# Moving the probability transposes of a fused attention and MoE kernel to float32r operands

## The chip, the cores and the metric

The program runs on one core of one Trainium2 chip. The metric is the device time of one execution in microseconds (us); smaller is better. The kernel before takes 770.42 us (median of three runs, 769.28 to 771.31).

## The reference

Attention over 2 batches, 8 heads, 768 positions and head size 64, in which a query sees only the keys whose 6-bit hash bucket equals its own; then a layer `g = h - tanh(h)` and a gated layer. In the core of it:

```python
mask = q_bucket[:, :, :, None] == k_bucket[:, :, None, :]
scores = np.where(mask, scale * np.matmul(q, k.transpose(0, 1, 3, 2)), -1000000000.0)
scores = scores - np.max(scores, axis=-1, keepdims=True)
attn = np.exp(scores)
attn = attn / (np.sum(attn, axis=-1, keepdims=True) + 1e-09)
x = np.matmul(attn, v)          # regrouped to 1536 tokens x 512
h = x @ w_in; x = (h - np.tanh(h)) @ w_out
g = x @ w_gate; out = (g * (1.0 / (1.0 + np.exp(-g))) * (x @ w_val)) @ w_out2
```

## The kernel before, in words

**Attention** takes the first 245 us or so of the span. The work is cut into 96 steps: 8 pairs of heads, 2 halves of the queries (384 columns each, `TB`), 2 heads of the pair, 3 blocks of 128 queries. `declare_step` declares one step:

- four score matmuls on TensorE (L835; float32r, 384 columns each) into one of two score buffers in PSUM (`s`), which already hold the mask;
- the row maximum on VectorE (L845), the exponential with the row sum on ScalarE (L847; it writes the probabilities into one of four slots `p`), the reciprocal of the sum (L851 on VectorE or GpSimd, L853 on VectorE), and the scaling of the slot in place on GpSimd (L854);
- six transposes of 128x128 on TensorE (L865, the function `transposes`): three into each of the two PSUM buffers `t`. A block of the slot is the stationary operand, an identity matrix of 128 columns is the moving one. Slot, identity and output are float32;
- two copies out of `t` into `pt`, on ScalarE or VectorE (L871).

Every six steps, `declare_pv` issues the product with `v` (L888, plain float32, 24 records for one half of a pair, in two bundles of 12). Its result goes to the feature tiles by L894. Beside the steps run the preparation of the next pair (hash matmul L798, one-hot matmul L832, L769, L787, the moves L745) and the blocks of the next layer's input (L550, L552, L557).

The slots `p` are the first 8 columns-blocks of one long tile, `ct_a`, which also holds the feature tiles from block `XF` = 8 on and is used again later by the matmuls of the layers (`ct_t`). In the profile all of these are called `ct`, and the identity is part of `csb`, which two DMAs of GpSimd's queue fill (L1157).

**The layers** follow: products of a Strassen-like scheme in float32r (L1044, 384 columns) and the second matmuls (L1098, 384 or 512 columns). Their weights arrive as 64-bit values and are converted by VectorE, GpSimd and ScalarE (L462 to L513); that begins while attention still runs.

**Order.** `Plan.order` takes each engine's list of operations from a table of numbers written into the file (`ORDER`). An engine works its list strictly in that order and waits where an operand isn't ready. On TensorE a step's transposes stand behind the scores of later steps, with bundles of the product with `v` in between. The operation as it is declared:

```python
op({"PE": 0.3275 * (1.0, SLOW)[i < 4]}, transposes, r=[pk, "ident"], w=[("t", z)], lat=0.2)
```

The number in it is the planner's cost of three transposes; where the table decides, it moves nothing.

Of the kernel before, what the change touches and what calls it, by code (L numbers as in the profile page):

```python
# [8 lines left out]
F32 = mybir.dt.float32  # L9
F32R = mybir.dt.float32r  # L10
# [4 lines left out]
ALU = mybir.AluOpType  # L15
# [3 lines left out]
NB, NH, S, D = 2, 8, 768, 64  # L19
NBITS = 6  # L20
NPAIR = NH // 2
TB = 384
# [10 lines left out]
NG, NC, NT = 16, 6, 11  # L33
# [13 lines left out]
def chunk_keys():  # L47
# [150 lines left out]
    POOL="""  # L198
# [34 lines left out]
class Plan:  # L233
# [15 lines left out]
    def op(self, eng, fn, r=(), w=(), due=0.0, lat=None, late=False, after=0.0, alt=None, port=()):  # L249
        n = len(self.ops)  # L250
        deps = set()
        for k in r:
            deps.update(self.writers.get(k, ()))
        for k in w:
            deps.update(self.writers.get(k, ()))
            deps.update(self.readers.get(k, ()))
        for k in r:
            self.readers.setdefault(k, []).append(n)
        for k in w:
            if k in r:  # L260
                self.writers.setdefault(k, []).append(n)
            else:
                self.writers[k] = [n]
                self.readers[k] = []
        deps.discard(n)
        self.banks[n] = {k[:2] for k in (*r, *w) if k[0] == "s"}
        eng = {e: t * (1 if e == "PE" or not self.n_first else self.SAFE) for e, t in eng.items()}
        self.ops.append((eng, fn, deps, due, self.LAT if lat is None else lat, late, after,
                         ALT if alt is None else alt, port, self.PE_WAIT if "PE" in eng else 0.0))
# [100 lines left out]
def lsh_attention_moe_kernel(ctx: ExitStack, tc: tile.TileContext, qT, kT, vP, proj, cst, wts, out):  # L370
    nc = tc.nc
    eng = {"PE": nc.tensor, "DVE": nc.vector, "ACT": nc.scalar, "POOL": nc.gpsimd, "SP": nc.sync}
    plan = Plan()
    op = plan.op

    def tiles(stack, name, n, shape, dtype=F32, **kw):
        pool = stack.enter_context(tc.tile_pool(name=name + "_p", bufs=n, **kw))
        return [pool.tile(shape, dtype, tag=name, name=name) for _ in range(n)]
# [10 lines left out]
    pw = fs[:, 2 * S:].bitcast(BF16).rearrange("p (j c) -> p j c", j=4)  # L389
# [11 lines left out]

    op_a = tiles(ctx, "op", 1, [128, 28 * TB], F32R)[0]
    op_t = [op_a[:, i * TB:(i + 1) * TB] for i in range(28)]
    ct_a = tiles(ctx, "ct", 1, [128, (NC + NT + 2) * TB])[0]
    ct_t = [ct_a[:, i * TB:(i + 1) * TB] for i in range(NC + NT + 2)]
    p_t = [ct_a[:, i * S:(i + 1) * S] for i in range(4)]
    XF = 8
    at = ExitStack()
    const = at.enter_context(tc.tile_pool(name="const", bufs=1))
    csb = const.tile([128, 262], F32, name="csb")  # L410
    ident = csb[:, 0:128]
    ones_b = csb[:, 128:129]
    bias_b = csb[:, 129:130]
    pj = const.tile([128, 32], F32, name="pj")
    x_t = tiles(ctx, "x", 1, [128, 512], space=PSUM)
    h_t = tiles(ctx, "h", 1, [128, 512], space=PSUM)
# [2 lines left out]
    t_t = tiles(ctx, "t", 2, [128, 512], space=PSUM)  # L419
# [5 lines left out]
    def ring(name, n):  # L425

        c = counts[name] = counts.get(name, -1) + 1
        return name, c % n
# [166 lines left out]
    def xf_at(half, p, n=1):  # L595
        return ct_a[:, (XF + 4 * half + p) * TB:(XF + 4 * half + p + n) * TB]

# [7 lines left out]
        return "xf", BLOCK[name][0], BLOCK[name][1] + k  # L605

    def tmp_at(ks):
        return ct_a[:, (NC + NT + ks[0]) * TB:(NC + NT + ks[0] + len(ks)) * TB]

    def tmp_key(k):  # L610
        return "tmp", k
# [4 lines left out]
    m_t = tiles(at, "m", 4, [128, 1])  # L616
    sm_t = tiles(at, "sm", 4, [128, 1])
    r_t = tiles(at, "r", 4, [128, 1])
# [203 lines left out]
    def declare_step(i, oh=None):  # L822
        n, half, e, qt = steps[i]
        sk = ring("s", 2)
        s = s_t[sk[1]]
        a, b, qk = ops_of["q", n, e, half]
        ks = [ops_of["k", n, e, kh] for kh in range(2)]
        q0 = slice(qt * 128, qt * 128 + 128)

        def qk_mm(g):  # L830
            if oh:
                g.matmul(out=h_t[0][:, 0:TB], lhsT=pw[:, 2 * oh[0] + oh[1], :], rhs=oh[2][0], start=True, stop=True)  # L832
            for first in (True, False):
                for kh in range(2):
                    g.matmul(  # L835
                        out=s[:, kh, 0:TB], lhsT=(b, a)[first][:, q0], rhs=ks[kh][0 if first else 1],
                        start=first, stop=not first,
                    )

        op({"PE": (0.87 if oh else 0.7) * (1.0, SLOW)[i < 6]}, qk_mm, r=qk + ks[0][2] + ks[1][2] + ([oh[2][1], "pw"] if oh else []),  # L840
           w=[sk + (0,), sk + (1,)] + ([("h", 0)] if oh else []), lat=0.25)
        sv = s[:, :, 0:TB]
        mk, smk, rk, pk = ring("m", 4), ring("sm", 4), ring("r", 4), ring("p", 4)
        m, sm, r, p = m_t[mk[1]], sm_t[smk[1]], r_t[rk[1]], p_t[pk[1]]
        op({"DVE": 0.87}, lambda g: g.tensor_reduce(out=m, in_=sv, axis=AX.XY, op=ALU.max, negate=True),  # L845
           r=[sk + (0,), sk + (1,)], w=[mk])
        op({"ACT": 0.9}, lambda g: g.activation(  # L847
            out=p.rearrange("p (a b) -> p a b", a=2), in_=sv, func=ACTF.Exp, bias=m, accum_out=sm
        ), r=[sk + (0,), sk + (1,), mk], w=[pk, smk])

        op({"DVE": 0.17, "POOL": 0.3}, lambda g: g.tensor_scalar(  # L851
            out=r, in0=sm, scalar1=1e-9, scalar2=None, op0=ALU.add), r=[smk], w=[rk])
        op({"DVE": 0.15}, lambda g: g.reciprocal(out=r, in_=r), r=[rk], w=[rk])  # L853
        op({"POOL": 0.91}, lambda g: g.tensor_scalar(  # L854
            out=p, in0=p, scalar1=r, scalar2=1.0, op0=ALU.mult, op1=ALU.mult
        ), r=[pk, rk], w=[pk])
        if qt == 0:
            pt_k[n, half, e] = ring("pt", 4)
        ptk = pt_k[n, half, e]
        pt = pt_t[ptk[1]]  # L860

        for z in range(2):
            def transposes(g, z=z):
                for kt in range(3):
                    g.transpose(out=t_t[z][:, kt * 128:(kt + 1) * 128], in_=p[:, z * TB + kt * 128:z * TB + (kt + 1) * 128], identity=ident)  # L865

            op({"PE": 0.3275 * (1.0, SLOW)[i < 4]}, transposes, r=[pk, "ident"], w=[("t", z)], lat=0.2)
            dst = pt[:, 3 * z:3 * z + 3, qt * 128:(qt + 1) * 128]
            src = t_t[z][:, 0:TB].rearrange("p (c q) -> p c q", c=3)
            op({"ACT": 0.4, "DVE": 0.47}, lambda g, dst=dst, src=src:  # L870
               g.activation(out=dst, in_=src, func=ACTF.Copy) if g is nc.scalar else g.tensor_copy(dst, src),  # L871
               r=[("t", z)], w=[ptk + (qt, z)])
# [39 lines left out]
        return i, k, w  # L912

    def ct_first(i):
        return [("p", i // 2)] if i < 8 else [("xf", (i - XF) // 4, (i - XF) % 4)] if i < 16 else []

    def c_slot():
        i, k, w = slot("c", NC, range(NC), ct_first)
        return ct_t[i], k, w
# [11 lines left out]
    def stage(layer, m):  # L931

        if m == 0:
            stages[layer] = ring(("st", layer), (2, 4)[layer - 1])[1]
        r = stages[layer]
        key = "st", layer, r, m
        size = (TB, DM)[layer - 1]
        first = []
        if key not in used:
            used.add(key)  # L940
            if layer == 1:
                first = [("xf", r, m)]
            else:
                first = [("acc", r // 2, 4 * (r % 2) + k) for k in range(m * DM // TB, ((m + 1) * DM - 1) // TB + 1)]
        if layer == 1:
            at_ = lambda n=1: ct_a[:, (8 + 4 * r + m) * TB:(8 + 4 * r + m + n) * TB]
        else:
            at_ = lambda n=1: late["acc"][r // 2][:, (r % 2) * 1536 + m * DM:(r % 2) * 1536 + (m + n) * DM]
        return at_, key, first
# [126 lines left out]
    def out_group(layer, i, sb, j):  # L1076
# [71 lines left out]
        if layer == 1 and i == NP1 - 1 and j == 7:  # L1148
            x_blocks(sb, [0, 1], lambda name, ks: acc_at(sb, ACC[name] + ks[0], len(ks)), lambda name, k: ("acc", sb, ACC[name] + k),
                     tmp_at, tmp_key, e + ZDUE[sb], True, MIX, 3)  # L1150
# [2 lines left out]
    MIX = [lambda n: {"DVE": dve(n), "POOL": pool(n)}] * 11  # L1153

    op({"ACT": 0.4}, lambda g: g.dma_start(out=pj, in_=proj), w=["pj"], due=-10, lat=2.5)
    for key, c in (("csb", slice(128, 262)), ("ident", slice(0, 128))):
        op({"POOL": 0.8}, lambda g, c=c: g.dma_start(out=csb[:, c], in_=cst[:, c]), w=[key], due=-10, lat=4.0)  # L1157

    def make_pw(g):
        for j in range(4):  # L1160
            g.tensor_scalar(
                out=pw[:, j, :], in0=csb[:, 130:258], scalar1=csb[:, 258 + j:259 + j], scalar2=None, op0=ALU.mult,
            )

    op({"DVE": 0.9}, make_pw, r=["csb"], w=["pw"], due=-5)
# [15 lines left out]
    for i in range(nst):  # L1181
        n, r = divmod(i, 12)
        m = (i + HASH_STEP) // 12
# [23 lines left out]
    for _, n, m in sorted(slots):  # L1207
        name, i, sb = units[n]
# [91 lines left out]
```

## Time and profile before

| | us |
|---|---|
| median of three runs | 770.42 (769.28 to 771.31) |
| profiled execution, first to last instruction (span) | 768.9 |
| TensorE busy | 754.3 |
| VectorE busy | 602.5 |
| ScalarE busy | 452.1 |
| GpSimd busy | 353.7 |

One execution was profiled. Its span is listed; what lay around the span in that same execution is not, so the difference from the median, 1.5 us, stands for it. Busy times are of records whose ends are modelled for matmuls, and a matmul's record overlaps with the next one's, so TensorE's share says that matmuls follow one another, not how closely. How closely is read from the distance between starts, or from the length of a bundle in the chain of waits, where overlaps are taken out. In the rows below PE is TensorE's matmul side, PEld its weight loads, DVE is VectorE, ACT ScalarE and POOL GpSimd.

### The profile page before, as it was taken

The numbers are of one execution on the slowest core, as the hardware profiler recorded it, in microseconds if no ns is written. First come the engines' busy times: TensorE is split into PE (matmuls) and PEld (weight loads), VectorE is DVE, ScalarE is ACT, GpSimd is POOL, SyncE is SP. The second block draws the span as 40 slices with busy tenths as digits, with TensorE's granted clock in tenths as the row PEclk, the third lists the DMA queues.
The fourth block names the chain that finished last, engine by engine and source line by source line (L and its number), as shares of the span: only waits on it lengthen the run. The fifth ranks groups of instructions, "written<-read, shape, count | busy, mean of one in ns | idle before, by whom it ended". The sixth has DMA issues, their size and how long they took to land.

```text
span 768.9 us, 12367 instructions
## 1 busy us (share of the span) xinstructions
PE 754.3 (98%) x4342; PEld 664.9 (86%) x4342; DVE 602.5 (78%) x1077; ACT 452.1 (59%) x955; POOL 353.7 (46%) x390
## 2 busy tenths in 40 slices
PE   7999999999999999999999999999999999999997
PEld 4677677776767999999999999999999998999896
DVE  6878777888897668888587889997785767789465
ACT  5787788878876646555555546656455443454220
POOL 5665657867785743223233353744135543323010
PEclk9999999999999999999999999999999999999999
DMA  6564465356323016788585763422347665587303
GB/s 172 140 182 93 128 180 137 91 131 176 120 83 110 29 27 174 170 191 198 120 191 123 194 146 91 107 88 91 124 147 185 147 121 140 126 187 159 78 14 150
DMA packets 37133, 101.09 MB, mean 131 GB/s; under 512 B 4656, under 2 KB 10032, under 8 KB 37072
## 3 DMA queue, kind: packets, MB, share of 16 engines
q1 hardware_dynamic: 28288, 71.06, 30.3%
q0 software_dynamic: 8320, 28.45, 20.9%
q10 hardware_dynamic: 464, 0.80, 0.5%
q8 instruction: 34, 0.56, 0.3%
q14 instruction: 27, 0.22, 0.1%
HBM read 49.17 MB, written 15.73 MB: 84 GB/s over the span
## 4 chain that ended last, share of the span: by engine, by line
PE 87%; DVE 4%; DMA 2%; ACT 2%; POOL 2%; issue 1%; SPq 0%; ACTq 0%; DVEq 0%; POOLq 0%
PE bs L1044 30%; PE t L1098 16%; PE s L835 8%; PE h L1098 8%; PE x L888 8%; PE t L865 7%; PE x L1098 6%; PE x L1044 2%; PE t L1044 2%; ACT ct L847 1%; POOL ct L854 1%; DMA q<-in_qT 1%; PE h L1044 1%; DMA raw<-in_w 1%; DVE ct L961 1%
## 5 line engine op out<-in xcount | busy, mean ns | idle before, releaser
L1044 PE MATMUL bs<-x,wi 128*128 128x384 f32 x1200 | 230.8, 335 | 1.4 <-DVE ct L1027 1.4
L1044 PEld LDWEIGHTS bs<-x,wi 128*128 128x128 f32 x1200 | 210.5, 188 | 6.2 <-DVE ct L1027 1.7
L854 POOL TENSOR_SCALAR ct<-ct,r 128x768 f32<-128x768 f32 x96 | 94.0, 983 | 30.5 <-DVE r L853 14.5
L845 DVE TENSOR_REDUCE m<-s 128x1 f32<-128x768 f32 x96 | 91.0, 952 | 20.9 <-PE s L835 19.4
L847 ACT ACTIVATE ct<-s,m 128x768 f32<-128x768 f32 x96 | 86.5, 902 | 17.7 <-DVE m L845 7.1
L835 PE MATMUL s<-op 128*128 128x384 f32 x384 | 91.7, 363 | 2.6 <-ACT ct L847 2.3
L1024 ACT ACTIVATE ct<-bs 128x384 f32<-128x384 f32 x120 | 57.0, 490 | 53.6 <-PE bs L1044 52.4
L865 PE MATMUL t<-csb,ct 128*128 128x128 f32 x576 | 82.1, 275 | 2.3 <-POOL ct L854 1.6
L865 PEld LDWEIGHTS t<-csb,ct 128*128 128x128 f32 x576 | 66.7, 140 | 18.5 <-POOL ct L854 5.5
L835 PEld LDWEIGHTS s<-op 128*128 128x128 f32 x384 | 63.7, 189 | 19.0 <-ACT ct L847 10.8
L871 ACT ACTIVATE pt<-t 128x384 f32<-128x384 f32 x133 | 61.2, 489 | 26.3 <-PE t L865 25.6
L1098 PE MATMUL t<-op,wo 128*128 128x384 f32 x384 | 75.7, 335 | 0.0
L888 PE MATMUL x<-pt,v 128*64 128x384 f32 x384 | 69.0, 495 | 0.0
L1098 PEld LDWEIGHTS t<-op,wo 128*128 128x128 f32 x384 | 67.2, 188 | 0.6 <-DVE ct L1129 0.3
L1098 PE MATMUL t<-wo,op 128*128 128x512 f32 x264 | 67.1, 393 | 0.0
L1137 POOL DMA_DIRECT2D acc<-ct x24 | 21.0, 887 | 78.7 <-ACT ct L1129 39.5
L1098 PEld LDWEIGHTS t<-wo,op 128*128 128x128 f32 x264 | 49.0, 188 | 8.3
L476 POOL TENSOR_TENSOR wi<-fs,wi 128x512 fp32r<-128x512 f32 (+1 forms) x25 | 39.8, 1595 | 25.9 <-ACT wi L474 25.8
L961 POOL TENSOR_TENSOR op<-ct,op 128x384 fp32r<-128x384 f32 x29 | 31.9, 1138 | 42.1 <-ACT op L966 32.9
L961 POOL TENSOR_TENSOR ct<-ct 128x384 f32<-128x384 f32 x24 | 26.4, 1100 | 52.8 <-ACT ct L980 31.9
L888 PEld LDWEIGHTS x<-pt,v 128*64 128x64 f32 x384 | 24.7, 136 | 28.6 <-issue 28.4
L474 ACT ACTIVATE wi<-fs 128x512 fp32r<-128x512 f32 (+1 forms) x60 | 41.8, 701 | 12.4 <-DVE fs L494 4.2
(170 smaller groups left out, 1412.1 us busy)
## 6 DMA issues: line engine op xcount, KB each, us to landing
raw<-in_w SPq DMA_DIRECT2D x68, 512.0 KB, 3.5
acc<-ct POOLq DMA_DIRECT2D x24, 768.0 KB, 6.3
out<-acc POOLq DMA_DIRECT2D x12, 768.0 KB, 8.1
op<-raw SPq DMA_DIRECT2D x42, 192.0 KB, 3.0
op<-f SPq DMA_DIRECT2D x56, 96.0 KB, 3.0
v<-in_v SPq DMA_DIRECT2D x8, 384.0 KB, 4.1
out<-acc SPq DMA_DIRECT2D x4, 768.0 KB, 4.6
acc<-out SPq DMA_DIRECT2D x4, 768.0 KB, 5.1
```

The costliest lines, as they stand in the source:

```text
L474: op({"ACT": act(n)}, lambda e: e.activation(out=hi, in_=src, func=ACTF.Copy), r=rk, w=[wk + (0,)], due=due, late=late)
L835: g.matmul(out=s[:, kh, 0:TB], lhsT=(b, a)[first][:, q0], rhs=ks[kh][0 if first else 1], start=first, stop=not first,)
L845: op({"DVE": 0.87}, lambda g: g.tensor_reduce(out=m, in_=sv, axis=AX.XY, op=ALU.max, negate=True), r=[sk + (0,), sk + (1,)], w=[mk])
L847: op({"ACT": 0.9}, lambda g: g.activation(out=p.rearrange("p (a b) -> p a b", a=2), in_=sv, func=ACTF.Exp, bias=m, accum_out=sm), r=[sk + ...
L854: op({"POOL": 0.91}, lambda g: g.tensor_scalar(out=p, in0=p, scalar1=r, scalar2=1.0, op0=ALU.mult, op1=ALU.mult), r=[pk, rk], w=[pk])
L865: g.transpose(out=t_t[z][:, kt * 128:(kt + 1) * 128], in_=p[:, z * TB + kt * 128:z * TB + (kt + 1) * 128], identity=ident)
L871: g.activation(out=dst, in_=src, func=ACTF.Copy) if g is nc.scalar else g.tensor_copy(dst, src),
L888: g.matmul(out=x[r, :], lhsT=v[:, kt, r], rhs=pt_t[ptks[e][1]][:, kt, :], start=(kt == 0), stop=(kt == NKT - 1), tile_position=(0, 64 * e),)
L961: op({"DVE": dve(TB), "POOL": pool(TB)} if port else {"DVE": dve(TB) + 0.01}, lambda e: e.tensor_tensor(out=now(dst), in0=now(a), in1=b, o ...
L1024: op({"ACT": act(TB)}, lambda e: e.activation(out=dst, in_=bank(), func=ACTF.Copy), r=[bk], w=dk, due=due)
L1044: e.matmul(out=bank(), lhsT=w[:, wpart, wi * 256 + k * 128:wi * 256 + k * 128 + 128], rhs=x_at(sb, xn, xpart, k), start=first and m == 0, ...
L1098: e.matmul(out=ps(), lhsT=lhs, rhs=rhs, start=c == 0, stop=c == 5)
```

## The change

The six transposes of a step take float32r operands and write float32r: the slot by a second name, the identity by a tile of its own, the output by a view. The four slots become buffers of their own. Each is placed twice at the same address, once as float32 (`p`, written by L847 and L854) and once as float32r (`pr`, read by the transposes). `ct_a` is shorter by the eight blocks that held the slots; `ct_t` still finds them as its first eight entries, and the places of the other entries are shifted to match (`XF`, `tmp_at`, `ct_first`, `stage`). The constants are loaded by the same two DMAs into two tiles, where one of them now goes from a float32 tensor into a float32r tile.

```diff
-    ct_a = tiles(ctx, "ct", 1, [128, (NC + NT + 2) * TB])[0]
-    ct_t = [ct_a[:, i * TB:(i + 1) * TB] for i in range(NC + NT + 2)]
-    p_t = [ct_a[:, i * S:(i + 1) * S] for i in range(4)]
-    XF = 8
+    base = -(-nc.sbuf_base // 32) * 32
+    nc.alloc_sbuf_tensor("arena", [128, 4 * S], F32)
+    p_t, pr_t = ([nc.alloc_sbuf_tensor_at("%s%d" % (n, i), [128, S], d, offset=base + 4 * S * i).ap() for i in range(4)]
+                 for n, d in (("p", F32), ("pr", F32R)))
+    ct_a = tiles(ctx, "ct", 1, [128, (NC + NT - 6) * TB])[0]
+    ct_t = [p_t[i // 2][:, (i % 2) * TB:(i % 2 + 1) * TB] for i in range(8)] + [ct_a[:, i * TB:(i + 1) * TB] for i in range(NC + NT - 6)]
+    XF = 0
...
-    csb = const.tile([128, 262], F32, name="csb")
-    ident = csb[:, 0:128]
-    ones_b = csb[:, 128:129]
-    bias_b = csb[:, 129:130]
+    csb = const.tile([128, 134], F32, name="csb")
+    ident = const.tile([128, 128], F32R, name="ident")
+    ones_b = csb[:, 0:1]
+    bias_b = csb[:, 1:2]
...
-        m, sm, r, p = m_t[mk[1]], sm_t[smk[1]], r_t[rk[1]], p_t[pk[1]]
+        m, sm, r, p, pr = m_t[mk[1]], sm_t[smk[1]], r_t[rk[1]], p_t[pk[1]], pr_t[pk[1]]
...
-                    g.transpose(out=t_t[z][:, kt * 128:(kt + 1) * 128], in_=p[:, z * TB + kt * 128:z * TB + (kt + 1) * 128], identity=ident)
+                    g.transpose(out=t_t[z][:, kt * 128:(kt + 1) * 128].bitcast(F32R), in_=pr[:, z * TB + kt * 128:z * TB + (kt + 1) * 128], identity=ident)
...
-    for key, c in (("csb", slice(128, 262)), ("ident", slice(0, 128))):
-        op({"POOL": 0.8}, lambda g, c=c: g.dma_start(out=csb[:, c], in_=cst[:, c]), w=[key], due=-10, lat=4.0)
+    for key, t, c in (("csb", csb, slice(128, 262)), ("ident", ident, slice(0, 128))):
+        op({"POOL": 0.8}, lambda g, t=t, c=c: g.dma_start(out=t, in_=cst[:, c]), w=[key], due=-10, lat=4.0)
```

No instruction moves: on every engine the same operations stand in the same order as before. On TensorE, where a step's transposes stand ahead of a bundle of the product with `v` (`ct` is the long tile, `csb` the constants, the number behind a name is a buffer's), it stood thus before:

```order
90 L835 MATMUL s0_112<-op_86 128x384 x4
91 L865 MATMUL t_108<-csb_94,ct_90 128x128 x3
92 L865 MATMUL t_107<-csb_94,ct_90 128x128 x3
93 L888 MATMUL x_99<-pt_131,v_120 64x384
94 L888 MATMUL x_99<-pt_132,v_120 64x384
```

and at the same place, with the change:

```order
90 L838 MATMUL s0_121<-op_86 128x384 x4
91 L868 MATMUL t_117<-ident_103,pr1_92 128x128 x3
92 L868 MATMUL t_116<-ident_103,pr1_92 128x128 x3
93 L891 MATMUL x_108<-pt_140,v_129 64x384
94 L891 MATMUL x_108<-pt_141,v_129 64x384
```

Only the operands of the transposes changed, and the line numbers by three.

## Rows read from the trace of the kernel before

**Rows 1.** The page's slices: busy tenths by engine, granted clock.

```profile
PE   7999999999999999999999999999999999999997
...
DVE  6878777888897668888587889997785767789465
ACT  5787788878876646555555546656455443454220
POOL 5665657867785743223233353744135543323010
PEclk9999999999999999999999999999999999999999
```

**Rows 2.** The page's chain that ended last, by engine and by line.

```profile
PE 87%; DVE 4%; DMA 2%; ACT 2%; POOL 2%; issue 1%; SPq 0%; ACTq 0%; DVEq 0%; POOLq 0%
PE bs L1044 30%; PE t L1098 16%; PE s L835 8%; PE h L1098 8%; PE x L888 8%; PE t L865 7%; PE x L1098 6%; PE x L1044 2%; PE t L1044 2%; ACT ct L847 1%; POOL ct L854 1%; DMA q<-in_qT 1%; PE h L1044 1%; DMA raw<-in_w 1%; DVE ct L961 1%
```

**Rows 3.** Busy time by stretch: start, pairs 2 to 7, end of attention, first layers.

```profile
core 0: us, PE busy (x) PEld busy (x) DVE busy (x) ACT busy (x) POOL busy (x), PEclk, DMA share, GB/s
13.00:69.00 56.00, 52.75 (x338) 37.07 (x339) 47.65 (x89) 42.87 (x94) 34.01 (x54) 1.00 0.53 135
69.00:213.00 144.00, 143.56 (x941) 103.26 (x939) 115.92 (x231) 121.23 (x265) 102.44 (x138) 1.00 0.50 134
213.00:242.00 29.00, 28.14 (x179) 22.26 (x176) 26.45 (x48) 19.19 (x43) 19.33 (x22) 1.00 0.28 93
...
300.00:500.00 200.00, 200.00 (x1152) 199.19 (x1151) 167.20 (x280) 113.02 (x237) 75.93 (x70) 1.00 0.64 153
```

**Rows 4.** The same stretches, transposes of L865 alone (PE, PEld).

```profile
13.00:69.00 56.00, 19.26 (x133) 15.36 (x134) 1.00 0.53 135
69.00:213.00 144.00, 53.71 (x384) 44.50 (x383) 1.00 0.50 134
213.00:242.00 29.00, 9.10 (x60) 6.86 (x60) 1.00 0.28 93
```

**Rows 5.** The transposes by line: duration ns min/median/max, and shape.

```profile
L865 PEld LDWEIGHTS t<-csb,ct x576: 137/140/145, 16.9 to 239.5; 128*128 128x128 f32 x192
L865 PE MATMUL t<-csb,ct x576: 270/272/332, 16.9 to 239.6; 128*128 128x128 f32 x192
```

**Rows 6.** Timeline near 105 us, PE and PEld: start, length, count.

```profile
104.75 0.75 PEld L865 LDWEIGHTS t<-csb,ct 128*128 128x128 f32 x6
104.92 0.82 PE L865 MATMUL t<-csb,ct 128*128 128x128 f32 x6
```

**Rows 7.** Chain of waits in order of time: attention, then the layers.

```profile
110.24 0.66 PE t L865 x6
...
111.05 0.70 PE s L835 x4
...
114.01 2.09 PE x L888 x12
...
658.00 3.12 PE bs L1044 x18
...
666.60 1.36 PE t L1098 x6
```

**Rows 8.** The same chain, shares of the stretch from 0 to 245 us by line.

```profile
by line: PE s L835 24.2%; PE x L888 23.0%; PE t L865 22.3%; ACT ct L847 3.4%; POOL ct L854 3.4%; issue 3.3%; DMA q<-in_qT 3.0%; PE bs L1044 2.6%; PE h L832 1.7%; PE h L798 1.6%; DVE m L845 1.5%; ACT pt L871 1.4%; DMA op<-raw 1.3%; POOL r L8
```

**Rows 9.** Timeline, two weight loads each after an idle PEld: transposes, then scores.

```profile
78.14 0.20 PEld L865 LDWEIGHTS t<-csb,ct 128*128 128x128 f32 x2 [0.60 <-POOL r L851]
104.11 0.30 PEld L835 LDWEIGHTS s<-op 128*128 128x128 f32 x2 [0.60 <-ACT ct L847]
```

**Rows 10.** Weight loads between 69 and 213 us by line and shape.

```profile
L835 PEld LDWEIGHTS s<-op 128*128 128x128 f32 x252 | 41.9, 189 | 10.7 <-ACT pt L871 5.5 <-ACT ct L847 4.4 <-issue 0.6
L888 PEld LDWEIGHTS x<-pt,v 128*64 128x64 f32 x252 | 16.2, 136 | 18.6 <-issue 18.5 <-ACT op L787 0.2
L798 PEld LDWEIGHTS h<-fs,pj 128*32 128x32 f32 x32 | 0.6, 108 | 0.7 <-issue 0.7
```

**Rows 11.** Who waited for whom between 69 and 213 us, ACT.

```profile
ACT pt L871 <- PE t L865: 13.7, 25, 1.1
ACT ct L847 <- DVE m L845: 2.1, 5, 1.0
ACT ct L847 <- DVE r L851: 1.8, 1, 1.8
ACT ct L847 <- DVE r L853: 1.6, 3, 1.0
```

**Rows 12.** The constants: first and last issue, and landing in us.

```profile
L1157 POOL DMA_DIRECT2D csb<-in_cst x2: 603/684/764, 1.3 to 8.9; - x2
...
csb<-in_cst POOLq DMA_DIRECT2D x1, 64.0 KB, 4.7
```

More of the change, by code (lines that the diff above doesn't have):

```diff
@@ L607, in tmp_at @@
     def tmp_at(ks):
-        return ct_a[:, (NC + NT + ks[0]) * TB:(NC + NT + ks[0] + len(ks)) * TB]
+        return ct_a[:, (NC + NT - 8 + ks[0]) * TB:(NC + NT - 8 + ks[0] + len(ks)) * TB]
     def tmp_key(k):
@@ L914, in ct_first @@
     def ct_first(i):
-        return [("p", i // 2)] if i < 8 else [("xf", (i - XF) // 4, (i - XF) % 4)] if i < 16 else []
+        return [("p", i // 2)] if i < 8 else [("xf", (i - 8) // 4, (i - 8) % 4)] if i < 16 else []
     def c_slot():
@@ L945, in stage @@
         if layer == 1:
-            at_ = lambda n=1: ct_a[:, (8 + 4 * r + m) * TB:(8 + 4 * r + m + n) * TB]
+            at_ = lambda n=1: ct_a[:, (4 * r + m) * TB:(4 * r + m + n) * TB]
         else:
@@ L1161, in make_pw @@
             g.tensor_scalar(
-                out=pw[:, j, :], in0=csb[:, 130:258], scalar1=csb[:, 258 + j:259 + j], scalar2=None, op0=ALU.mult,
+                out=pw[:, j, :], in0=csb[:, 2:130], scalar1=csb[:, 130 + j:131 + j], scalar2=None, op0=ALU.mult,
             )
```

## The prediction

> **What bounds the kernel now.** I read the slices first, for where the engines are full [rows 1]. TensorE is at nine tenths or more from the second slice on and its granted clock is at full rate throughout, so the change can neither lose nor win through the clock. The other engines are nearly as full as it only in the first twelve slices, the attention. Then the chain that ended last [rows 2]: 87% of it is TensorE, and the transposes of L865 are 7% of the span. Cut to attention, they are 22.3% of 245 us, that is 54.6 us [rows 8]. A saving on them is therefore a saving on the path, as long as no other engine takes TensorE's place.
>
> Whether one would, the stretches tell [rows 3]. Between 69 and 213 us TensorE has matmul records in 143.56 of 144 us, ScalarE is busy for 121.23, VectorE for 115.92, GpSimd for 102.44. Before 69 us VectorE is at 47.65 of 56, and after 213 us at 26.45 of 29, where it converts the layers' weights as well. The layers behind attention are TensorE's alone (200.00 of 200 us), so what attention gains, the end gains.
>
> **The price of a transpose now.** A record lasts 272 ns [rows 5], but records overlap. Six of them last 0.82 us together [rows 6], so starts are (0.82 - 0.272) / 5 = 0.110 us apart, and the chain, where overlaps are out, has 0.66 / 6 = 0.110 for one as well [rows 7]. All 576 [rows 5] come to 63.4 us, of which the 54.6 on the chain are 86%.
>
> **The price after.** No row has a float32r transpose, so I bound it. For float32r matmuls the chain has 3.12 us for 18 of 384 columns, 0.1733 each, and 1.36 us for 6 of 512 columns, 0.2267 each [rows 7]. 128 columns more cost 0.0533 us; what is left after three times that is 0.0134 us per instruction. A float32 transpose at 0.110 is about twice 0.0533: its 128 columns go through at half the rate. If float32r gives the transpose the whole rate, as it has it in the scores, 128 columns cost 0.0533 + 0.0134 = 0.067 us, and the change saves 0.043 us on each, 24.8 us over 576.
>
> The weight load could stand in the way, since every transpose loads its own block. From the two loads that start after an idle queue, one load's own length off, starts are 0.20 - 0.14 = 0.06 us apart for the transposes and 0.30 - 0.19 = 0.11 us for the scores [rows 5, 9, 10]. Which of the two will a float32r transpose have? Plain float32 loads of 32 and 64 columns last 108 and 136 ns [rows 10]; at 28 ns per 32 columns, 128 would last 192, as the float32r loads of the scores do with 189. So outside transposes the two types load alike, and what makes a transpose's load 140 instead of 190 is that it is a transpose, which it stays. I take 0.06, which hides behind 0.067. The other end, 0.11, would leave nothing of the saving.
>
> The Trainium skill (TensorE: Matmul & The Clock Gate, LDWEIGHTS) gives a load's time as its columns divided by 1.2, which is 107 ns for 128 columns, and in its section on weight-path modes it keeps the faster load from float32. By that rule transposes are bound by their loads already, another type for them saves nothing, and the sum would be 770.4 us. The scores' 0.11 us agrees with it; the transposes' 0.06 us does not [rows 9].
>
> **What of it reaches the end.** At most the chain's share: 86% of 24.8 is 21.3 us. It is less, because the engines' lists are fixed and the others fill in.
>
> - 69 to 213 us: 384 transposes [rows 4], 16.5 us at stake. ScalarE is idle for 144 - 121.2 = 22.8 us there, 13.7 of it waiting for transposes [rows 11]. Faster transposes can remove those waits; the other 9.1 us (for maxima, reciprocals and scalings) remain or grow. So this stretch can hardly fall below 130 us, a saving of 14. TensorE also waits for ScalarE already, 5.5 + 4.4 us in front of the scores [rows 10], and such waits grow as it comes earlier: a score buffer is free only after L847, a `t` buffer only after L871. I take 9 us, a bit over half.
> - 13 to 69 us: 133 records [rows 4], 5.7 us at stake. VectorE is at 85% there and TensorE stands idle for 3 us [rows 3]. I take 2.5.
> - 213 to 242 us: 60 records, 2.6 us at stake, VectorE at 91%. I take 0.5.
>
> Sum: 12 us. The span of 768.9 becomes 756.9; with the 1.5 us by which the median stood above it, 758.4 us.
>
> **What costs nothing.** The copies of L871 read the same bytes from the same buffers. The scaling of L854 writes the same slot under its first name, so its length stays, and the transposes still wait for it. The identity's DMA is issued at 8.9 us and took 4.7 to land, at 13.6, and the first transpose starts at 16.9 [rows 5, 11, 12], a cover of 3.3 us. Now that DMA changes the type; were it twice as slow, it would come 1.4 us too late, once, beside other waits. The shifted places move no work. A few waits in the layers come from other earlier operations, but TensorE's lists there are unbroken [rows 3]. Nothing is queued behind a new wait, for no instruction gets a new one in attention.
>
> **The rivals.**
>
> *The loads or a fixed latency set the pace: no change.* If the float32r block loads as the scores' do, 0.11 us [rows 9], transposes come as far apart as now. For it: no row has a load of float32r as short as 140 ns. Against it: the lengths of plain float32 loads above. Time: 770.4 us. The Trainium skill (same page, PE-mode transpose) holds a transpose in a kernel to be mostly access latency, some 275 ns; records here are that long, but 0.110 us apart, so latency isn't what they are spaced by.
>
> *A float32r transpose keeps the half rate and pays the type's own cost: slower.* All four bytes have to pass through in a transpose, so the array may take 128 columns at half the rate as now, 2 x 0.0533, and add the 0.0134 us that every float32r matmul has over its columns: 0.120 us. (A load of 0.11 plus the same 0.0134 comes to 0.124.) That is 0.010 more for each, 5.8 us, of which 86 to 100% is on the path: some 776 us. It decides if the cost after is above 0.110. For it: the transpose in float32 has half the rate where a single pass might have been expected. The far end is the plain float32 matmul: the product with `v` needs 2.09 us for 12 records that run two side by side [rows 7], 0.35 per 384 columns and record, with two records for each product; a third of 0.70 is 0.23 us for 128 columns, and a float32r transpose treated so would add some 70 us in all. Nothing in the rows points there.
>
> *One pass, but the steps don't close up.* If the work of ScalarE and VectorE and their waits for each other set the pace of a step as soon as TensorE doesn't, less than 2.3 us reach the end: 768 to 770 us. Against it: ScalarE's 13.7 us of waits for transposes [rows 11].
>
> **How the numbers follow.** Forecast (0.067 us or somewhat more, half of it realised): 0.63. Its own range goes from 749 (all of the chain's 21.3 us) to 766 (0.080 us for one, a quarter realised). Load or latency as now 0.14, one pass without effect 0.05: 0.19 for no change. Slower 0.18, of which 0.04 are for the far end. A difference under 0.3%, 2.3 us, can't be told from none. The range has to reach across no change and into the slower case: 749 to 775 leaves out under 0.2.
>
> **What would show it.** In the changed profile, six transposes of one step should last 0.40 us instead of 0.66 in the chain, two loads after an idle queue still 0.20 us. The transposes' share of attention's chain should fall from 22% to about 15%, ScalarE's wait for transposes should shrink, and its busy share between 69 and 213 us should rise to about 90%. Transposes 0.11 or 0.12 us apart would make the forecast wrong at its first step; 0.067 apart with the layers starting no earlier would make it wrong at the second.

## The result, and the profile after

| | before | with the change |
|---|---|---|
| median, us (4 runs each) | 770.87 (769.28 to 771.46) | 763.38 (761.92 to 764.73) |
| ratio, 95% interval | | 0.9904 (0.9885 to 0.9924) |
| span of the profiled execution, us | 768.9 | 762.3 |

The change makes the kernel faster by 7.5 us, about 1%. The page of the changed kernel has the chain that ended last, as [rows 2] had it:

```profile
PE 81%; POOL 6%; DVE 6%; issue 2%; DMA 2%; ACT 2%; SPq 0%; POOLq 0%; DVEq 0%; ACTq 0%
PE bs L1047 30%; PE t L1101 16%; PE h L1101 8%; PE x L891 6%; PE s L838 6%; PE x L1101 6%; PE t L868 3%; PE x L1047 2%; POOL p L857 2%; PE t L1047 2%; DVE m L848 1%; ACT p L850 1%; DMA raw<-in_kT 1%; POOL x L555 1%; PE h L1047 1%
```

TensorE's share fell from 87% to 81%, GpSimd's and VectorE's rose to 6% each. The transposes are L868 now and went from 7% of the span to 3%. The same chain cut to attention, 0 to 240 us, by line (it answers to [rows 8]):

```profile
by line: PE x L891 19.1%; PE s L838 18.9%; PE t L868 11.1%; POOL p L857 7.8%; issue 7.2%; DVE m L848 4.7%; ACT p L850 4.0%; DMA raw<-in_kT 3.5%; POOL x L555 3.1%; PE bs L1047 2.7%; POOL r L854 2.0%; PE h L835 1.5%; DMA op<-raw 1.3%; DVE pt 
```

The transposes lost half their share (22.3% to 11.1%). The scores and the product with `v`, whose work is unchanged, lost about a fifth of theirs: for part of attention TensorE isn't what is waited for any longer. In their place stand GpSimd's scaling (3.4% before, 7.8% now), VectorE's maximum (1.5%, now 4.7%) and issue.

The price of a transpose, in the chain in order of time (as [rows 7]) and by line (as [rows 5]):

```profile
110.43 0.46 PE t L868 x6
110.89 2.09 PE x L891 x12
```

```profile
L868 PEld LDWEIGHTS t<-ident,pr x576: 137/140/151, 17.4 to 233.4; 128*128 128x128 f32 x192
L868 PE MATMUL t<-ident,pr x576: 221/247/284, 17.5 to 233.5; 128*128 128x128 f32 x192
```

Six take 0.46 us instead of 0.66, 0.077 for one instead of 0.110. The last one starts at 233.5 us instead of 239.6. Busy time in the stretches of [rows 3], with the middle one cut at 207 us, and the transposes alone in the same stretches:

```profile
13.00:69.00 56.00, 50.77 (x346) 36.10 (x347) 48.78 (x91) 43.42 (x95) 35.48 (x55) 1.00 0.54 136
69.00:207.00 138.00, 135.00 (x934) 95.96 (x933) 115.72 (x231) 120.10 (x263) 101.81 (x138) 1.00 0.53 140
```

```profile
13.00:69.00 56.00, 15.62 (x138) 14.17 (x138) 1.00 0.54 136
69.00:207.00 138.00, 41.94 (x378) 38.62 (x378) 1.00 0.53 140
```

The columns after the times are PE, PEld, DVE, ACT and POOL in the first, PE and PEld in the second. TensorE, full before, is without a matmul for 3 of 138 us now. A step in the middle takes 138 x 6 / 378 = 2.19 us, before 144 x 6 / 384 = 2.25.

Behind attention the layers kept their length. The first and the last product of the layers, of the kernel before and then with the change:

```profile
L1044 PE MATMUL bs<-x,wi x1200: 331/334/443, 229.5 to 752.4; 128*128 128x384 f32 x172
```

```profile
L1047 PE MATMUL bs<-x,wi x1200: 333/334/444, 223.4 to 745.9; 128*128 128x384 f32 x172
```

They start 6.1 us earlier and end 6.5 us earlier.

### The profile page after: what moved, and what is told of

It reads as the page before. It is cut to its first block, busy times and chain, and to the rows that moved or that the text cites. A ratio compares the mean times of both kernels' runs of the same rounds, so it can differ in the third digit from the quotient of the medians.

```text
span 762.3 us, 12361 instructions
## 1 busy us (share of the span) xinstructions
PE 744.4 (98%) x4342; PEld 656.0 (86%) x4342; DVE 601.5 (79%) x1077; ACT 451.6 (59%) x955; POOL 354.1 (46%) x390
## 4 chain that ended last, share of the span: by engine, by line
PE 81%; POOL 6%; DVE 6%; issue 2%; DMA 2%; ACT 2%; SPq 0%; POOLq 0%; DVEq 0%; ACTq 0%
PE bs L1047 30%; PE t L1101 16%; PE h L1101 8%; PE x L891 6%; PE s L838 6%; PE x L1101 6%; PE t L868 3%; PE x L1047 2%; POOL p L857 2%; PE t L1047 2%; DVE m L848 1%; ACT p L850 1%; DMA raw<-in_kT 1%; POOL x L555 1%; PE h L1047 1%
## 5 line engine op out<-in xcount | busy, mean ns | idle before, releaser
L857 POOL TENSOR_SCALAR p<-p,r 128x768 f32<-128x768 f32 x96 | 94.6, 989 | 25.5 <-DVE r L856 15.5
L850 ACT ACTIVATE p<-s,m 128x768 f32<-128x768 f32 x96 | 86.6, 903 | 20.2 <-DVE m L848 12.1
L1027 ACT ACTIVATE p<-bs 128x384 f32<-128x384 f32 x120 | 57.0, 490 | 54.1 <-PE bs L1047 52.7
L868 PEld LDWEIGHTS t<-ident,pr 128*128 128x128 f32 x576 | 59.1, 140 | 22.9 <-POOL p L857 8.0
L874 ACT ACTIVATE pt<-t 128x384 f32<-128x384 f32 x133 | 61.2, 489 | 17.7 <-PE t L868 17.2
L868 PE MATMUL t<-ident,pr 128*128 128x128 f32 x576 | 64.9, 245 | 5.5 <-POOL p L857 3.2
L1047 PE MATMUL bs<-op,wi 128*128 128x384 f32 x240 | 47.2, 335 | 0.5 <-DVE ct L964 0.5
L1047 PEld LDWEIGHTS bs<-op,wi 128*128 128x128 f32 x240 | 42.1, 188 | 1.4 <-DVE ct L964 1.0
```

Source lines behind the costliest of these rows:

```text
L850: op({"ACT": 0.9}, lambda g: g.activation(out=p.rearrange("p (a b) -> p a b", a=2), in_=sv, func=ACTF.Exp, bias=m, accum_out=sm), r=[sk + ...
L857: op({"POOL": 0.91}, lambda g: g.tensor_scalar(out=p, in0=p, scalar1=r, scalar2=1.0, op0=ALU.mult, op1=ALU.mult), r=[pk, rk], w=[pk])
L868: g.transpose(out=t_t[z][:, kt * 128:(kt + 1) * 128].bitcast(F32R), in_=pr[:, z * TB + kt * 128:z * TB + (kt + 1) * 128], identity=ident)
L1027: op({"ACT": act(TB)}, lambda e: e.activation(out=dst, in_=bank(), func=ACTF.Copy), r=[bk], w=dk, due=due)
L1047: e.matmul(out=bank(), lhsT=w[:, wpart, wi * 256 + k * 128:wi * 256 + k * 128 + 128], rhs=x_at(sb, xn, xpart, k), start=first and m == 0, ...
```

## The experiments

The question is what one transpose saves and why not all of it came through. Times are medians; "the change" is 763.4 us, and each batch had its own runs of the kernel before (770.6 to 771.4 us), so differences between batches are good to about 1 us.

### Type or buffers?

```diff
-    ident = const.tile([128, 128], F32R, name="ident")
+    ident = const.tile([128, 128], F32, name="ident")
...
-                    g.transpose(out=t_t[z][:, kt * 128:(kt + 1) * 128].bitcast(F32R), in_=pr[:, z * TB + kt * 128:z * TB + (kt + 1) * 128], identity=ident)
+                    g.transpose(out=t_t[z][:, kt * 128:(kt + 1) * 128], in_=p[:, z * TB + kt * 128:z * TB + (kt + 1) * 128], identity=ident)
```

> The change without the type: slots as buffers of their own, identity as a tile of its own, but slots, identity and output of the transposes float32. Theory (the whole gain is the shorter transpose): starts of transposes 0.110 us apart again, chain 0.66 us for six, time as before, 770.9 us within 0.3%. Rival (the own buffers or the other layout give part of it): below 768.5 us. Rival (they cost something that the type hides): above 773 us.

770.94 us, ratio to before 0.9998 (0.9988 to 1.0008), and six transposes take 0.66 us in its chain again. The own buffers, the shifted places and the second tile of constants are worth nothing. All of the gain is the type's.

### The price where TensorE alone binds

```diff
-                for kt in range(3):
+                for kt in (0, 0, 1, 1, 2, 2):
```

> The change, with every transpose issued twice in a row (1152 float32r transposes; the second repeats the first). All other work stays. Theory (one costs 0.085 us by the distance of its weight loads, and with twelve of them per step TensorE binds attention again): 576 more cost close to 49 us, less what TensorE waited for before, 800 to 812 us. Rival (one costs about 0.067 us in a long row, as the prediction had it): under 798 us.

> The kernel before, with every transpose issued twice in a row (1152 float32 transposes at 0.110 us). Theory (the saving per transpose is 0.025 us and it is worth its whole size where TensorE alone binds): 826 to 834 us, and the distance to the same edit of the change is 1152 x 0.025 = 29 us, 25 to 32. Rival (half of any saving on transposes is swallowed whatever binds): a distance of about 15 us.

The change with doubled transposes: 798.16 us. The kernel before with doubled transposes: 826.07 us. The chain in order of time, scores that follow a row of twelve transposes and the next row, first of the change so edited, then of the kernel before:

```profile
104.10 0.77 PE s L838 x4
104.87 0.97 PE t L868 x12
```

```profile
101.34 0.70 PE s L835 x4
102.04 1.31 PE t L865 x12
```

In a long row one transpose takes 0.97 / 12 = 0.081 us in float32r and 0.109 in float32. Each of the six that were added costs (0.97 - 0.46) / 6 = 0.085 us and (1.31 - 0.66) / 6 = 0.108 us. Not all of the difference is saved: the scores behind a row take 0.77 us of the chain in float32r and 0.70 in float32. Scores and row together differ by 0.27 us, 0.022 for each transpose, and where the product with `v` follows (2.09 us in both) it is 0.34 us, 0.028 for each.

The two kernels lie 27.9 us apart, within the 25 to 32 expected, 0.024 us for each of the 1152 transposes. Counted in the two traces, from the start of the last matmul ahead of each row to the start of the first one behind it, the rows differ by 28.1 us in all. So where TensorE is full, the whole saving reaches the end, and a transpose saves 0.024 us, 14 us over the 576 of the kernel. The 0.033 that the chain's rows of six show (0.110 less 0.077) is too much.

The total of the change so edited was below the 800 us expected: 576 more transposes at 0.085 us are 49 us of work and cost 34.8 us, so some 14 us of them went where TensorE had been waiting. Before, 62 us of work cost 55.2, so 7 us went there. TensorE's waits thus grew with the change by about 7 us, which is the half of the 14 that didn't come through.

### Is TensorE still the bound?

```diff
-                for kt in range(3):
+                for kt in range(1):
```

> The change, with one transpose of three left out twice: a step transposes one block into each t buffer instead of three (the other two thirds of pt keep old contents), 192 instead of 576. TensorE loses 384 transposes at about 0.08 us, 31 us of work; all other work stays. Theory (half of the saving was lost because ScalarE, VectorE and GpSimd take over the chain): they take over more, the time falls by 4 to 15 us, to 748 to 759 us. Rival (attention is still bound by TensorE and the saving was lost elsewhere): it falls by 25 us or more, to 738 us or less.

760.11 us: 31 us less work for TensorE gave 3.3 us, less even than the theory's 4. Its busy time by stretch, columns as above:

```profile
13.00:69.00 56.00, 48.62 (x256) 30.31 (x255) 48.25 (x90) 42.99 (x95) 34.87 (x55) 0.92 0.53 135
69.00:207.00 138.00, 124.08 (x691) 76.58 (x689) 117.35 (x236) 119.45 (x266) 103.48 (x140) 0.99 0.53 140
```

Between 69 and 207 us TensorE has no matmul for 14 of 138 us, where the change has 3, and VectorE, ScalarE and GpSimd do hardly more in that time than in the change. The granted clock is 0.92 in the first stretch, a mean of 2.4 GHz and some 1.2 GHz, with TensorE idle for 7 of 56 us there; in the long middle stretch it is 0.99. That took back some of the gain. The four executions go from 759.09 us at a mean clock of 0.995 to 761.94 at 0.988, so by estimate some 3 us would come on top at the full clock. Even so only a fifth of the 31 us would have reached the end: attention is no longer TensorE's, and a still shorter transpose is worth little.

### Which engine took its place?

In the change and in the kernel before:

```diff
-            out=p, in0=p, scalar1=r, scalar2=1.0, op0=ALU.mult, op1=ALU.mult
+            out=p[:, 0:1], in0=p[:, 0:1], scalar1=r, scalar2=1.0, op0=ALU.mult, op1=ALU.mult
```

> The change, with the scaling on GpSimd cut to the first column of the slot (the other columns stay unscaled): same waits, GpSimd does 96 times about 0.1 us instead of 0.98. Theory (GpSimd's scaling, with 7.8% of the changed attention's chain, is one of the works that took TensorE's place): 4 to 10 us less than the change, 753 to 759 us. Rival (ScalarE or the fixed lists bind, GpSimd only stands beside them): within 2 us of 763.4.

> The kernel before, with the same cut of the scaling to one column. Theory (before, TensorE bound attention between 69 and 213 us and GpSimd stood in the chain with 3.4% of 245 us, mostly at its ends): 2 to 5 us less than before, 766 to 769 us, and less than the same cut brings after the change. Rival (GpSimd cost as much before as after): the same fall in both.

758.09 us (5.3 less than the change) and 767.92 us (3.0 less than before). Both as the theories expected, though a single column takes 0.32 us, not 0.1. GpSimd's scaling cost the change more than it had cost the kernel before, and without most of it the type is worth 9.8 us instead of 7.5. It isn't the only one: 9.8 is still short of the 14 that TensorE saves.

Then more of the same work, by an edit that was meant to help, with `pr` in the change and `p` before as the slot's name for the output:

```diff
-        op({"POOL": 0.91}, lambda g: g.tensor_scalar(
-            out=p, in0=p, scalar1=r, scalar2=1.0, op0=ALU.mult, op1=ALU.mult
-        ), r=[pk, rk], w=[pk])
+        def scaling(g):
+            for lo, hi in ((0, TB), (TB, S)):
+                g.tensor_scalar(out=pr[:, lo:hi], in0=p[:, lo:hi], scalar1=r, scalar2=1.0, op0=ALU.mult, op1=ALU.mult)
+        op({"POOL": 0.91}, scaling, r=[pk, rk], w=[pk])
```

> The change, with GpSimd's scaling of a slot cut into two instructions of 384 columns that write the slot by its float32r name, so that a step's first three transposes wait for the first half alone. GpSimd's work stays about as it is (a scaling of 384 columns elsewhere in the trace takes 0.50 us, two of them 1.0 against 0.98). Theory (transposes wait for GpSimd's scaling, which comes late; earlier by half a scaling): 1 to 4 us less than the change, 759.5 to 762.5 us. Rival (GpSimd's throughput counts, not when half a slot is ready): the same as the change or slower.

> The kernel before, with the scaling cut into the same two halves. Theory (there the transposes seldom waited for the scaling): within 1.5 us of before. Rival: as much gain as in the change.

779.71 us and 777.29 us: both theories missed, by their price for a half. With the change the time lies where its rival had it (slower); before, neither came true. Groups by line on GpSimd, 69 to 207 us, of the change so edited and of the one with the scaling in one piece by the float32r name:

```profile
L859 POOL TENSOR_SCALAR pr<-p,r 128x384 fp32r<-128x384 f32 x120 | 77.1, 646 | 13.9 <-DVE r L856 3.6 <-ACT x L553 2.0 <-DVE r L854 0.4
```

```profile
L859 POOL TENSOR_SCALAR pr<-p,r 128x768 fp32r<-128x768 f32 x63 | 61.1, 974 | 16.8 <-DVE r L856 10.2 <-DVE r L854 2.6 <-PE s L838 2.1
```

Two halves take 1.29 us, not 1.0, so GpSimd is busy for 0.32 us more per step. The times rose by 16.3 us in the change and by 6.4 before, but the two edits weren't the same dose. The two halves of one step in GpSimd's timeline, of the change so edited and then of the kernel before:

```profile
100.90 1.27 POOL L859 TENSOR_SCALAR pr<-p,r 128x384 fp32r<-128x384 f32 x2 [0.71 <-DVE r L856]
```

```profile
101.00 1.16 POOL L857 TENSOR_SCALAR ct<-ct,r 128x384 f32<-128x384 f32 x2 [0.37 <-DVE r L853]
```

A half lasts 0.59 us in both by the median, 0.65 and 0.64 by the mean. In the change the second half waits for the first in every step and starts 0.09 us after its end; before, it starts 0.02 us ahead of that end. So a step holds GpSimd for about 0.41 us more in the change and 0.28 us more before, 39 and 27 us over 96 steps, of which 41% and 24% show in the time. GpSimd's work still weighs more with the change, by less than the bare times say. Halves written in the change by the name `p` were not run, so whether the second name brings the wait stays open. The chain of the change so edited, 0 to 255 us, by line:

```profile
by line: POOL pr L859 21.2%; issue 11.7%; PE s L838 10.9%; PE x L893 10.6%; PE t L870 8.0%; PE bs L1049 3.8%; DVE m L848 3.6%; SPq L748 3.3%; POOL r L854 3.2%; POOL x L555 3.1%; DMA q<-in_qT 2.8%; DMA op<-raw 2.3%; DVE pt L876 2.1%; POOL ct
```

```diff
-            out=p, in0=p, scalar1=r, scalar2=1.0, op0=ALU.mult, op1=ALU.mult
+            out=pr, in0=p, scalar1=r, scalar2=1.0, op0=ALU.mult, op1=ALU.mult
```

> The change, with the scaling in one piece but written by the slot's float32r name (it is then rounded as it is written). Theory (the form of the write costs GpSimd nothing): within 1.5 us of the change, 762 to 765 us. Rival (writing float32r costs more on GpSimd, or the waits fall differently): 2 us or more away.

763.82 us, the same as the change. In one piece the name by which the slot is written costs nothing, so the halves, with the wait between them, were the cause. By the time for which a step's scaling holds GpSimd:

| a step's scaling, us of GpSimd | before | with the change | the type's worth |
|---|---|---|---|
| 0.32 (one column) | 767.92 | 758.09 | 9.8 |
| 0.98 (as it is) | 770.87 | 763.38 | 7.5 |
| two halves (means): 1.26 before, 1.39 with the change | 777.29 | 779.71 | -2.4, not like for like |

### Taking work off GpSimd

The additions of L854 that the list has on GpSimd, moved to VectorE (in the change and before), and every fourth scaling, moved likewise (in the change), by editing the lists before they are used:

```diff
+        for n, o in enumerate(ops):
+            if len(o[0]) == 2 and abs(o[0].get("POOL", 0) - 0.3) < 1e-9 and n in ORDER["POOL"]:
+                ORDER["POOL"].remove(n)
+                ORDER["DVE"].insert(ORDER["DVE"].index(n + 1), n)
```

> The change, with the small additions to the row sums that the list gives to GpSimd moved to VectorE, each right before its reciprocal (GpSimd loses some 60 of 0.235 us, VectorE gains as many of 0.146). Theory (GpSimd's way through sum, reciprocal and scaling holds the transposes up): 1 to 4 us less than the change, 759 to 762 us. Rival (VectorE, busy for 121 of 144 us in the middle of attention, is as much a bound): the same or up to 4 us more than the change.

> The kernel before, with the same move. Theory (there TensorE had cover for GpSimd's way): within 1.5 us of before. Rival (it shortens every step's way): 2 us less or more.

764.44 us in the change and 772.02 us before (ratio 1.0008, 0.9998 to 1.0018): no gain in either. Before, that is what the theory had; in the change it lies in the rival's range, by which VectorE pays what GpSimd is spared.

```diff
-        op({"POOL": 0.91}, lambda g: g.tensor_scalar(
+        op({"POOL": 0.91, "DVE": 0.5}, lambda g: g.tensor_scalar(
...
+        for i, n in enumerate([n for n, o in enumerate(ops) if o[0].get("POOL", 0) == 0.91 and o[0].get("DVE", 0) == 0.5]):
+            if i % 4 == 3:
+                ORDER["POOL"].remove(n)
+                ORDER["DVE"].insert(ORDER["DVE"].index(n - 1) + 1, n)
```

> The change, with every fourth scaling (24 of 96) on VectorE, right behind its reciprocal, instead of on GpSimd. A version that might beat both kernels. GpSimd loses 24 x 0.98 = 23.5 us, a quarter of what the cut to one column took off it, which gave 5.3 us; VectorE gains some 24 x 0.5 us (estimated from its 0.43 us for a scaling of 512 columns in the weights). Theory (GpSimd's late scalings are the largest single thing that took TensorE's place): 1 to 3 us less than the change, 760.5 to 762.5 us. Rival (VectorE, 115.7 of 138 us busy, pays it back, since maxima queue behind the scalings): the same as the change, or up to 3 us more.

768.14 us (765.99 to 769.72), 4.8 more than the change, worse than theory and rival. Groups by line on VectorE, 69 to 207 us, and the chain from 0 to 240 us by line:

```profile
L861 DVE TENSOR_SCALAR p<-p,r 128x768 f32<-128x768 f32 x15 | 10.7, 711 | 0.7
```

```profile
by line: PE s L842 21.2%; PE x L895 17.6%; PE t L872 12.1%; DVE m L852 9.6%; issue 5.6%; ACT p L854 4.1%; DVE pt L878 4.0%; POOL p L861 2.5%; PE bs L1051 2.4%; PE x L1182 2.1%; DVE op L776 2.0%; DVE p L861 1.8%; PE h L839 1.6%; DVE r L860 1
```

A scaling takes VectorE 0.71 us in the mean, not the 0.5 I had estimated. GpSimd's scaling left the chain (7.8 to 2.5%), and VectorE's maxima took its place (4.7 to 9.6%). No version here that does all of the work beats the change.

## Why the prediction came out as it did

The time lay in the range, on the side forecast, at 7.5 us of gain instead of 12.

**The bound.** Right: attention was TensorE's, and what it gained the layers passed on, 6.1 us at their start and 6.5 at their end.

**The price after: mis-sized.** The prediction took 0.067 us for a float32r transpose, from the columns at the full rate and 0.0134 for the instruction. It is 0.077 in the chain's rows of six, where 0.067 was to show as 0.40 us and 0.46 came, and each further one in a long row costs 0.085. By the doubled kernels one saves 0.024 instead of 0.043, 14 us over 576 instead of 24.8. The term that was too small is, as far as the rows show, the weight load: the prediction took the 0.06 us that it had read from the float32 transposes [rows 9] and hid it behind the 0.067. The first two loads after an idle queue, in the timeline of the change:

```profile
77.02 0.22 PEld L868 LDWEIGHTS t<-ident,pr 128*128 128x128 f32 x2 [0.60 <-POOL r L854]
```

With one load's 0.14 off, their starts are 0.08 us apart, where the float32 pair had 0.06; over all such pairs of the two traces it is 0.082 to 0.086 in float32r and 0.056 to 0.062 in float32. The 0.085 of a long row is the same distance, so float32r transposes follow one another as fast as their loads, while float32 transposes, at 0.109, are slower than theirs. That the load is the cause is read from this agreement. No run changed the load alone, and the first transpose's matmul has begun when the second load starts, so it may have a part in the distance. The distance lies between the two ends that the prediction had named, 0.06 and 0.11. That a transpose's load keeps its own form was right (its record still lasts 140 ns), that the type plays no part in its pace was not. Whether the columns themselves would pass in 0.067 can't be seen behind the loads.

The Trainium skill (TensorE: Matmul & The Clock Gate, LDWEIGHTS), with a load's columns divided by 1.2, would have 107 ns here. The traces have about 60 for float32 and 84 for float32r transposes, so the rule holds for the scores alone.

**What reaches the end: right in size.** The prediction had half of the saving come through (12 of 24.8); 7.5 of 14 did. So the gain is smaller than forecast by the price and not by the share. In the timelines the same rows of transposes start, before and then with the change:

```profile
68.92 0.82 PE L865 MATMUL t<-csb,ct 128*128 128x128 f32 x6
214.09 0.82 PE L865 MATMUL t<-csb,ct 128*128 128x128 f32 x6
```

```profile
68.00 0.63 PE L868 MATMUL t<-ident,pr 128*128 128x128 f32 x6
207.59 0.63 PE L868 MATMUL t<-ident,pr 128*128 128x128 f32 x6
```

At 69 us 0.9 us was gained, against 2.5 predicted; between the two rows 5.6, against 9; and behind them, to the last transpose, 0.4 was lost again, against a gain of 0.5. With 384 x 0.024 = 9.2 us at stake, the middle stretch passed on 60%, where the prediction had 55%.

One reading behind that share was wrong. The 5.5 + 4.4 us for which TensorE was said to wait for ScalarE already [rows 10] are idle times of the weight loads, under which matmuls went on. The matmul side waited for ScalarE, between 69 and 213 us before and between 69 and 207 us with the change:

```profile
PE s L835 <- ACT ct L847: 0.2, 1, 0.2
```

```profile
PE s L838 <- ACT p L850: 1.7, 7, 0.4
```

Such waits did grow, but from next to nothing. That the share came out right is in part luck.

**Who comes next.** The prediction named ScalarE, then VectorE, and had GpSimd only among those for whom ScalarE waits. ScalarE's waits in the middle stretch, as [rows 11]:

```profile
ACT pt L874 <- PE t L868: 7.4, 15, 1.1
ACT p L850 <- DVE m L848: 3.9, 10, 0.8
```

The transposes' share of attention's chain fell to 11%, below the 15% foreseen. ScalarE's wait for them fell from 13.7 to 7.4 us as foreseen, but it isn't full: 120.1 of 138 us, 87% instead of the 90% foreseen. GpSimd, busy for 101.8 of 138 us, 74%, has more of the chain. Each scaling stands behind a sum and a reciprocal, on which GpSimd waits (10.2 us for the reciprocals of L856 in the middle stretch, in the run that writes `pr` in one piece), so it can be late with time to spare. Shown is that its work weighs more with the change: 5.3 us against 3.0 when 0.66 us per step are taken away, and 41% against 24% of what the halves add. That the rest is shared by VectorE's maxima and ScalarE is read from the chain and from the two moves to VectorE; no run took it apart.

**What was held to cost nothing.** Right: 770.94 us with all of it but the type. The identity, whose DMA changes the type now, was issued at 8.6 us and took 5.4 instead of 4.7 to land, at 14.0, ahead of the first transpose at 17.4. That one came 0.5 us later than before; with the old type it starts at 17.7, so the type isn't the reason.

**The rivals.** Loads as slow as the scores' (0.11) and half the rate plus the type's own 0.0134 (0.120) are out at 0.081 to 0.085. Steps that don't close up at all are out too, at 7.5 us.

## What to carry to other kernels

Here TensorE was full and the next engines were busy for 71 to 84% of the same stretch. The first 14 us saved on it were worth half, and the next 31 a tenth to a fifth. The next bound need not be the next busiest engine: look for the one whose work stands late in a step's chain. A quick way to see what a saving is worth is to double the cheaper and the dearer form alike and compare the distance of the two times; lengths of single pieces of a chain can mislead, since part of a saving is handed on to the piece behind. Before two edits are compared as equal doses, compare what they did to the engine. And price a changed instruction by all of its parts: here the new pace was that of the weight loads, which had changed with the type.

## What the runs showed of the hardware that was not expected

- A transpose of 128 columns in a long row: 0.109 us in float32, 0.081 in float32r, where each further one costs 0.085. Two weight loads after an idle queue start 0.06 and 0.08 us apart, though each record lasts 0.14 in both.
- GpSimd's scaling of 768 columns takes 0.97 us and of 384 columns 0.65 (a single column 0.32), so halves of an instruction aren't halves in time; the 0.50 that a scaling by a constant takes for 384 columns was no guide. A second half that waits for the first starts 0.09 us after its end, one that doesn't 0.02 us before it.
- Leaving matmuls out went with a lower clock. With two of three transposes left out TensorE had no matmul for 3.4 of the 10 us between 20 and 30 us, and the granted clock was 0.78 between 30 and 35 us, a mean of 2.4 and 1.2 GHz; the change had none for 2.3 of the same 10 us, and its clock stayed at 1.00.
